# Eight heads of a decode step's forward part: sums of V with P times K as two products of 64 rows each

## The chip, the cores and the metric

The kernel runs on one core of one Trainium2 chip. The metric is the device time of one execution in microseconds (us); of the kernel before there are three such times, 1683.71, 1685.32 and 1685.54, with the median 1685.32.

## The reference

The kernel computes the forward and the backward of one decode step: layer norm, attention of one query per batch row over a cache of 4096 keys and values, an output projection with a residual, a second layer norm and a gated feed-forward block. It returns the output and the gradients, those of the K and V caches among them. Cut to what matters:

```python
B, Sq, D = 4, 1, 512;  H, Sk, Dh = 32, 4096, 128;  F = 1792
q = (layernorm(x) @ wq) as (B, H, 1, Dh)
scores = einsum("bhqd,bhkd->bhqk", q, k_cache) * Dh ** -0.5
p = softmax(scores)
o = einsum("bhqk,bhkd->bhqd", p, v_cache)
h = x + o @ wo
out = h + swiglu(layernorm(h), w1, w3, w2)
# and the vjp of out for grad_out: gradients of x, k_cache, v_cache, wq, wo, w1, w3, w2
```

There are 4 x 32 = 128 pairs of batch row and head, called heads here. Each has 1 MB of K and 1 MB of V in bf16.

## The kernel before

**Stages.** A forward part walks over the 128 heads and reads all of K and V (256 MB); it ends at about 660 us. A short middle part does the feed-forward block, forward and backward. The backward part reads V again and writes the gradients of K and V, 1 or 2 MB per transfer, until the end.

**Slots.** K, V, transposed K and P times K all live in one arena of 23 slots of about 1 MB each (`Slot`). A load is issued on the queue of SyncE (SP) as soon as a slot is given back. So the number of loads under way depends on how soon the engines release slots. One slot in every 16 heads goes for good to the results `M_of(s)`.

**What a head needs.** For head s, `T_pe` (TensorE, a quarter) and `T_dve` (VectorE, the rest) transpose K. `S_head` makes the scores in PSUM. The softmax goes through `sm_max`, `sm_max_T`, `sm_gmax`, `sm_bcast`, `sm_exp`, `sm_sum`, `sm_norm` and `sm_P`, for two heads at once. `PK_pairs` (GpSimd) and `PK_mul` (VectorE, line 460) multiply K by P. `M_mm` (line 475) sums over the 4096 keys the product of V with [P times K, P]: 32 matmuls, each with a 128x128 piece of V as weights and 130 columns of P times K, into one PSUM tile `M_ps` of 128x130. Its first 128 columns serve the gradients later, its 129th is the attention output. `M_end` adds up the rows of P times K with eight matmuls (line 485), lets ScalarE copy the tile to the arena (line 489), and gives the slots of P times K and V back. The pool `psM` has two buffers, both of tag "M".

**Order of the work.** The forward loop runs over 64 groups `gi` of two heads. Its order is written out by hand, and each engine runs its instructions in that order. In group gi the scores are those of heads 2gi and 2gi+1. The sums of V are those of two earlier heads: m1 = 2gi - 3 and m2 = 2gi - 2. On VectorE a group is, in order: `sm_max`, a transpose for the next group, `sm_gmax`, a transpose, the copy `nm` of `sm_exp` (line 422), the place of M_end(m1), two transposes, the reciprocal of `sm_norm`, PK_mul(pk1), the place of M_end(m2), a transpose of 1024 words (`T_dve(nb, 2, 2)`), and PK_mul(a). The part of the loop around the two M_end:

```python
        sm_exp(gi)
        if has1:
            M_end(m1)
...
        if has2:
            M_mm(m2, 24, SJ)
            M_end(m2)
            load_V(m2 + VQ)
...
            T_dve(nb, 2, 2)
        PK_mul(a)
```

Every 16 heads `O_cols` (lines 505 and 507) follows M_end(m1); its first copy on VectorE reads what ScalarE's copy of M_end(m1) has just written. Every 32 heads `kP_flush` follows too. Both are in the kernel before and after.

Of the kernel before, what the change touches and what calls it, by code (L numbers as in the profile page):

```python
# [9 lines left out]
FP32 = mybir.dt.float32  # L10
BF16 = mybir.dt.bfloat16
ALU = mybir.AluOpType
# [10 lines left out]
NPAIR = 8  # L23
OLD = 9
LEAD = 64


@with_exitstack
def kernel(
# [22 lines left out]
    nc = tc.nc  # L52
    P = nc.NUM_PARTITIONS
# [5 lines left out]
    Dh = A_k_cache.shape[3]  # L59
# [6 lines left out]
    SJ = Sk // P  # L66
# [3 lines left out]
    PKW = Dh + 2  # L70
# [55 lines left out]
    class Slot:  # L126
        def __init__(self, name, src=free):
# [5 lines left out]
            self.w = arena[:, self.i * SLOT:(self.i + 1) * SLOT]  # L133
            o = (self.i + 1) % 2 * LEAD
            self.t = self.w[:, o:o + SJ * Dh]
# [13 lines left out]
    class Slot2:  # L149
# [5 lines left out]
        def __init__(self):  # L155
            self.i = min(self.choices())[1]
            free.remove(self.i)
            free.remove(self.i + 1)
            self.t = arena[:, self.i * SLOT + LEAD:(self.i + 2) * SLOT]

# [56 lines left out]
    def ones_window(col):  # L217
        i = col % 2
        return onesw[i][:, 32 - i - col:64 - i - col]
# [80 lines left out]
    with ExitStack() as c0:  # L300
# [11 lines left out]
        for h in range(H):  # L312
            for cc in range(DC):
                nc.tensor.matmul(qT_ps[:, h, :], lhsT=wq_s[cc].b(HD)[:, h * Dh:(h + 1) * Dh], rhs=xhatT[:, cc, :],
                                 start=(cc == 0), stop=(cc == DC - 1))
# [4 lines left out]
        for r in range(2):  # L320
            for t_ in range(2):
                for q in range(4):
                    nc.tensor.matmul(qr_ps[32 * q:32 * (q + 1), 2 * r + t_, :], lhsT=ident_b[:, 64 * r + t_:64 * (r + 1):2],
                                     rhs=qT_bf[:], start=True, stop=True, tile_position=(0, 32 * q))
# [5 lines left out]
    def M_of(s):  # L330
        return Ms[s // MC].w[:].bitcast(FP32)[:, 0:MC * (Dh + 1)].rearrange("p (n c) -> p n c", c=Dh + 1)[:, s % MC, :]
# [3 lines left out]
    psM = c1.enter_context(tc.tile_pool(name="psM", bufs=2, space=bass.MemoryType.PSUM))  # L335
# [13 lines left out]
    hold = {}  # L349
# [103 lines left out]
    def PK_pairs(s):  # L453
        PKs[s] = Slot("PK")
        PK = PKs[s].w[:].rearrange("p (j c) -> p j c", c=PKW)
        nc.gpsimd.tensor_copy(out=PK[:, :, Dh:PKW], in_=P_all[:, s, :, None].to_broadcast([P, SJ, 2]))  # L456

    def PK_mul(s):
        PK = PKs[s].w[:].rearrange("p (j c) -> p j c", c=PKW)
        nc.vector.tensor_tensor(  # L460
            out=PK[:, :, 0:Dh].rearrange("p j (r t) -> p j r t", t=2),
            in0=Ks[s].heads().rearrange("p j (r t) -> p j r t", t=2),
            in1=PK[:, :, None, Dh:PKW].to_broadcast([P, SJ, Dh // 2, 2]),
            op=ALU.mult,
        )
        Ks.pop(s).give()
        kdone["n"] += 1

    def M_mm(s, j0, j1):
        if j0 == 0:  # L470
            hold["M"] = psM.tile([P, PKW], FP32, name="M_ps", tag="M")
        PK = PKs[s].w[:].rearrange("p (j c) -> p j c", c=PKW)
        Vn = Vs[s].heads()
        for j in range(j0, j1):
            nc.tensor.matmul(hold["M"][:], lhsT=Vn[:, j, :], rhs=PK[:, j, :], start=(j == 0), stop=(j == SJ - 1))  # L475

    def M_end(s):
        w = s % 32
        PK = PKs[s].w[:].rearrange("p (j c) -> p j c", c=PKW)
        if w == 0:  # L480
            hold["kP"] = psK.tile([P, 4, Dh], FP32, name="kP_ps", tag="kP")
        for c in range(2):
            for q in range(4):
                j0 = (c * 4 + q) * 4
                nc.tensor.matmul(hold["kP"][32 * q:32 * (q + 1), :, :], lhsT=ones_window(w), rhs=PK[:, j0:j0 + 4, 0:Dh],  # L485
                                 start=(w == 0 and c == 0), stop=(w == 31 and c == 1), tile_position=(0, 32 * q))
        if s % MC == 0:
            Ms.append(Slot("M"))
        nc.scalar.copy(out=M_of(s), in_=hold["M"][:, 0:Dh + 1])
        PKs.pop(s).give()  # L490
        Vs.pop(s).give()

# [160 lines left out]
    for gi in range(NGI):  # L653
        nxt = gi < NGI - 1
        a, na, nb = gi * G, gi * G + 2, gi * G + 3
# [6 lines left out]
        if has1:  # L662
            M_mm(m1, 0, 16)
# [6 lines left out]
        if has1:  # L670
            M_mm(m1, 16, SJ)
# [5 lines left out]
        if has1:  # L677
            M_end(m1)
            load_V(m1 + VQ)
            if m1 % 32 == 31:  # L680
                kP_flush(m1)
            if m1 % MC == MC - 1 and m1 < NH - 1:
                O_cols(m1 - MC + 1, m1 + 1)
# [15 lines left out]
        if has2:  # L699
            M_mm(m2, 0, 24)  # L700
        sm_P(gi)
# [4 lines that stand above are left out]
# [21 lines left out]
    PK_pairs(NH - 1)  # L727
    M_mm(NH - 3, 0, SJ)
    M_end(NH - 3)
    PK_mul(NH - 1)  # L730
    weights(NGI)
# [118 lines left out]
    with ExitStack() as cm:  # L850
# [40 lines left out]
        for wi, wt in enumerate((w1, w3)):  # L891
            for fc in range(FC):
                for cc in range(DC):
                    nc.tensor.matmul(gu_ps[:, wi, fc, :], lhsT=w13_view(wt, cc)[:, fc * P:(fc + 1) * P], rhs=hhatT[:, cc, :],
                                     start=(cc == 0), stop=(cc == DC - 1))
            if wi == 0:
# [13 lines left out]
                                in1=of4[:, :, None].to_broadcast([NH, B, Dh]), op=ALU.mult)  # L910
# [13 lines left out]
        for jj in range(DC):  # L924
            i_mm = 0
            for (lt, wt) in ((d_gateT_bf, w1), (d_upT_bf, w3)):
                for fc in range(FC):
                    nc.tensor.matmul(dn_ps[:, jj, :], lhsT=w13_view(wt, jj)[:, fc * P:(fc + 1) * P], rhs=lt[:, fc, :],
                                     start=(i_mm == 0), stop=(i_mm == 2 * FC - 1))
# [16 lines left out]
        for s in range(3):  # L946
# [8 lines left out]
                         start=True, stop=True)  # L955
# [5 lines left out]
                                       in1=hhatT_f[:], op0=ALU.mult, op1=ALU.mult)  # L961
        nc.vector.tensor_tensor(out=u[:], in0=u[:], in1=z[:, 0], op=ALU.add)
        nc.vector.scalar_tensor_tensor(out=u[:], in0=m[:, 0, None, :].to_broadcast([P, DC, B]), scalar=-1.0 / D,
                                       in1=u[:], op0=ALU.mult, op1=ALU.add)
# [5 lines left out]
        for b0, b1 in ((0, 1), (1, B)):  # L970
            ps = psA.tile([P, B, Dh], FP32, tag="rT", name="rep_ps")
            for b in range(b0, b1):
                for jj in range(DC):
                    nc.tensor.matmul(ps[:, b, :], lhsT=dhT[:, jj, b:b + 1].to_broadcast([P, P]), rhs=wo_page(0)[:, 0, jj, :],
                                     start=(jj == 0), stop=(jj == DC - 1))
# [12 lines left out]
    with ExitStack() as c2:  # L988
# [544 lines left out]
        for t in range(NT):  # L1533
            s = SP + 2 * t
# [46 lines left out]
```

## Time and profile before

| | |
|---|---|
| median of the three runs | 1685.32 us |
| the profiled execution's own time | 1683.33 us |
| its span, first to last instruction | 1681.5 us |
| busy: TensorE, VectorE, ScalarE, GpSimd | 74%, 74%, 57%, 25% of the span |
| data moved | 707.16 MB, 421 GB/s in the mean |
| the 128 `M_mm`: TensorE | 4096 matmuls, 285.9 us busy |
| the 128 `PK_mul`: VectorE | 292.4 us busy, 2285 ns each |
| span 240 to 260 us: TensorE, VectorE busy | 17.29 and 19.00 of 20 us |

The profile gives busy time, idle time and what ended it ("releaser", named by engine, tile and line). A line such as L475 is a line of the kernel before. PE is TensorE's matmuls, PEld its weight loads, DVE VectorE, ACT ScalarE, POOL GpSimd, SP SyncE. The timeline lists instructions in order of time: start and length in us, engine, line, operation, output and input, count, and in brackets the idle time before and what ended it.

### The profile page before, as it was taken

What the parts mean: (1) busy time and instruction counts of PE and PEld (TensorE: products, weight loads), DVE (VectorE), ACT (ScalarE), POOL (GpSimd) and SP (SyncE); (2) the same over time, 40 slices, a digit from 0 to 9 for tenths busy, and PEclk for the clock granted to TensorE, in tenths of its full rate; (3) what the DMA queues carried; (4) which work ended last, traced back from release to release, by engine and by line L of the source; (5) the groups of instructions that cost most, each with busy time, mean ns of one, the idle gap of its engine ahead of it and who ended that gap; (6) DMA issues with size and microseconds to landing.
All of it is one profiled execution on the core that took longest, in us unless ns stands there. A gap on an engine that the chain in (4) does not pass through costs nothing.

```text
span 1681.5 us, 33231 instructions
## 1 busy us (share of the span) xinstructions
PE 1243.9 (74%) x13784; PEld 874.1 (52%) x13784; DVE 1238.8 (74%) x1204; ACT 957.5 (57%) x1482; POOL 412.9 (25%) x732
## 2 busy tenths in 40 slices
PE   5889888888888888877777657567766776776750
PEld 4777776667666776644433335444444443444430
DVE  5989899999999987767766467576655656655682
ACT  3455454445445544677666556666665676676650
POOL 1221222222232223444552323211100011111110
PEclk9999999999999999999999878886667667676675
DMA  9999999999999999999999999999999999999996
GB/s 401 424 425 425 425 424 425 424 425 424 418 424 412 424 404 407 412 409 425 426 426 428 430 430 429 429 430 430 430 430 429 431 429 431 430 429 429 431 431 277
DMA packets 80983, 707.16 MB, mean 421 GB/s; under 512 B 8748, under 2 KB 12984, under 8 KB 15296
## 3 DMA queue, kind: packets, MB, share of 16 engines
q1 hardware_dynamic: 80416, 704.94, 99.4%
q8 instruction: 108, 1.77, 0.4%
q14 instruction: 43, 0.35, 0.0%
q0 software_dynamic: 416, 0.10, 0.0%
HBM read 422.59 MB, written 282.34 MB: 419 GB/s over the span
## 4 chain that ended last, share of the span: by engine, by line
DMA 40%; DVE 8%; PE 5%; ACT 4%; issue 3%; POOL 2%; DVEq 0%; SPq 0%; ACTq 0%; POOLq 0%
DMA out_dram<-arena 37%; DVE arena L1434 6%; ACT arena L806 3%; DMA arena<-in_A_v_cache_dram 3%; POOL zd L1246 1%; PE pt_tps L805 1%; PE M_ps L475 1%; DVE arena L460 1%; PE dq_ps L1032 1%; PE dP_ps L1280 1%; DMA arena<-arena 0%; PE pt_wo L613 0%; POOL P L1251 0%; ACT Pn L439 0%; POOL arena L1431 0%
## 5 line engine op out<-in xcount | busy, mean ns | idle before, releaser
L806 ACT COPY arena<-pt_tps 128x1024 bf16<-128x1024 bf16 x512 | 491.1, 1026 | 239.2 <-PE pt_tps L805 236.1
L805 PE MATMUL pt_tps<-ident_f,arena 128*128 128x128 f32 x2048 | 397.0, 346 | 195.4 <-DMA arena<-in_A_v_cache_dram 111.7
L805 PEld LDWEIGHTS pt_tps<-ident_f,arena 128*128 128x128 f32 x2048 | 290.8, 175 | 362.7 <-issue 187.3
L1434 DVE TENSOR_TENSOR arena<-arena 128x8192 bf16<-128x8192 bf16 x48 | 212.4, 4425 | 206.6 <-DMA out_dram<-arena 176.3
L475 PE MATMUL M_ps<-arena 128*128 128x130 bf16 x4096 | 285.9, 222 | 43.7 <-DMA arena<-in_A_v_cache_dram 43.2
L460 DVE TENSOR_TENSOR arena<-arena 128x4096 bf16<-128x4096 bf16 x128 | 292.4, 2285 | 24.3 <-POOL arena L456 24.3
L475 PEld LDWEIGHTS <-arena 128*128 128x128 bf16 x4096 | 252.3, 99 | 65.1 <-DMA arena<-in_A_v_cache_dram 58.1
L1434 DVE TENSOR_TENSOR arena<-dS,arena 128x8192 bf16<-128x8192 bf16 x48 | 212.4, 4426 | 63.6 <-DMA out_dram<-arena 63.6
L367 DVE STREAM_TRANSPOSE arena<-arena 128x512 f32<-128x512 f32 (+1 forms) x321 | 250.5, 796 | 0.0
L362 ACT COPY arena<-pt_tps 128x1024 bf16<-128x1024 bf16 x128 | 129.4, 1012 | 189.4 <-PE pt_tps L361 147.4
L373 POOL TENSOR_TENSOR W<-qrep,wmask 128x128 bf16<-128x128 bf16 x128 | 120.0, 938 | 85.6 <-PE S_ps L393 71.2
L1431 POOL COPY arena<-arena 128x128 bf16<-128x128 bf16 x48 | 45.2, 941 | 374.5 <-DVE arena L1434 248.6
L456 POOL COPY arena<-P_all 128x64 bf16<-128x64 bf16 x128 | 32.4, 253 | 413.1 <-ACT P_all L450 410.0
L1343 POOL COPY arena<-arena 64x4 bf16<-64x4 bf16 x96 | 78.5, 818 | 127.7 <-PE dP_ps L1363 118.2
L1363 PE MATMUL dP_ps<-arena 128*32 128x512 bf16 x768 | 85.3, 478 | 8.4 <-ACT arena L806 7.9
L450 ACT COPY P_all<-pt_P 32x64 bf16<-32x64 bf16 x256 | 51.9, 203 | 54.6 <-PE pt_P L446 52.4
L820 DVE TENSOR_TENSOR arena<-dS,arena 128x4096 bf16<-128x4096 bf16 x32 | 73.3, 2292 | 12.7 <-DMA out_dram<-arena 12.3
L361 PE MATMUL pt_tps<-ident_b,arena 128*128 128x128 bf16 x1024 | 80.5, 223 | 0.0
L820 DVE TENSOR_TENSOR arena<-P,arena 128x4096 bf16<-128x4096 bf16 x29 | 66.4, 2293 | 18.4 <-DMA out_dram<-arena 17.3
L485 PE MATMUL kP_ps<-arena,onesw 128*32 128x512 bf16 x1024 | 79.6, 388 | 0.0
L393 PE MATMUL S_ps<-arena,W 128*32 128x256 bf16 x1536 | 75.2, 286 | 0.5 <-DVE arena L367 0.2
L439 ACT ACTIVATE Pn<-E,rl 128x1024 bf16<-128x1024 f32 x64 | 73.7, 1151 | 3.2 <-DVE rl L436 3.2
(257 smaller groups left out, 1402.3 us busy)
## 6 DMA issues: line engine op xcount, KB each, us to landing
out_dram<-arena SPq DMA_DIRECT2D x96, 2048.0 KB, 27.5
arena<-in_A_v_cache_dram SPq DMA_DIRECT2D x160, 1024.0 KB, 15.9
arena<-in_A_k_cache_dram SPq DMA_DIRECT2D x128, 1024.0 KB, 15.5
arena<-in_A_v_cache_dram SPq DMA_DIRECT2D x48, 2048.0 KB, 31.7
out_dram<-arena SPq DMA_DIRECT2D x72, 1024.0 KB, 19.8
arena<-in_A_wq_dram SPq DMA_DIRECT2D x8, 1024.0 KB, 17.8
arena<-in_B_w_dram SPq DMA_DIRECT2D x8, 896.0 KB, 14.9
out_dram<-arena SPq DMA_DIRECT2D x6, 896.0 KB, 26.5
```

What stands on the lines that cost most here:

```text
L361: nc.tensor.transpose(pt[:, i, :], Kn[:, c * GW + i, :], ident_b[:])
L362: nc.scalar.copy(out=KT[:, c * GW:(c + 1) * GW, :], in_=pt[:])
L367: nc.vector.transpose(out=KT[:, c * w_:(c + n) * w_], in_=Kn[:, c * w_:(c + n) * w_])
L373: nc.gpsimd.tensor_tensor(out=W[:, hl], in0=qrep[:, :, s:s + 1].to_broadcast([P, 4, 32]), in1=wmask[:, hl, None, :].to_broadcast([P, 4, 32 ...
L460: nc.vector.tensor_tensor(out=PK[:, :, 0:Dh].rearrange("p j (r t) -> p j r t", t=2), in0=Ks[s].heads().rearrange("p j (r t) -> p j r t", t=2),
L475: nc.tensor.matmul(hold["M"][:], lhsT=Vn[:, j, :], rhs=PK[:, j, :], start=(j == 0), stop=(j == SJ - 1))
L485: nc.tensor.matmul(hold["kP"][32 * q:32 * (q + 1), :, :], lhsT=ones_window(w), rhs=PK[:, j0:j0 + 4, 0:Dh], start=(w == 0 and c == 0), stop ...
L805: nc.tensor.transpose(ptw[:, jj, :], w[:, 4 * g + jj, :], ident_f[:])
L806: nc.scalar.copy(out=v.rearrange("p (j d) -> p j d", d=Dh)[:, g * GW:(g + 1) * GW, :], in_=pt[:])
L820: nc.vector.tensor_tensor(out=dst.rearrange("p j (r t) -> p j r t", t=2), in0=col2[:, :, None, :].to_broadcast([P, SJ, Dh // 2, 2]), in1=r ...
L1363: nc.tensor.matmul(rows["acc"][32 * c:32 * (c + 1), :], lhsT=zt[t % B][:, k, ZP - m:ZP - m + 32], rhs=words_of(v, 2 * c + u, k), start=(pl ...
L1434: nc.vector.tensor_tensor(out=dst.rearrange("p (j r t) -> p j r t", r=Dh // 2, t=2), in0=col2[:, :, None, :].to_broadcast([P, 2 * SJ, Dh / ...
```

## The change

For heads 40 to 47 (`HALVES`) the 128 rows of the contraction are split. Each of the 32 steps becomes two matmuls, one over partitions 0 to 63 of V and of P times K, one over partitions 64 to 127, each placed in its own 64 rows of the array. The first sums into `M_ps`, the second into a second PSUM tile `Mh_ps`, taken from the same pool. After ScalarE's copy of `M_ps` VectorE adds the 129 columns of `Mh_ps` to the copied row. The other 120 heads are as before. The order of all other instructions on all engines, and of all transfers, is the same.

```diff
+HALVES = range(40, 48)
...
     def M_mm(s, j0, j1):
         if j0 == 0:
             hold["M"] = psM.tile([P, PKW], FP32, name="M_ps", tag="M")
+            if s in HALVES:
+                hold["Mh"] = psM.tile([P, PKW], FP32, name="Mh_ps", tag="M")
         PK = PKs[s].w[:].rearrange("p (j c) -> p j c", c=PKW)
         Vn = Vs[s].heads()
         for j in range(j0, j1):
+            if s in HALVES:
+                for a, M in enumerate((hold["M"], hold["Mh"])):
+                    r_ = slice(64 * a, 64 * (a + 1))
+                    nc.tensor.matmul(M[:], lhsT=Vn[r_, j, :], rhs=PK[r_, j, :], start=(j == 0), stop=(j == SJ - 1),
+                                     tile_position=(64 * a, 0))
+                continue
             nc.tensor.matmul(hold["M"][:], lhsT=Vn[:, j, :], rhs=PK[:, j, :], start=(j == 0), stop=(j == SJ - 1))
...
         nc.scalar.copy(out=M_of(s), in_=hold["M"][:, 0:Dh + 1])
+        if s in HALVES:
+            nc.vector.tensor_tensor(out=M_of(s), in0=M_of(s), in1=hold["Mh"][:, 0:Dh + 1], op=ALU.add)
```

## The prediction

> **What bounds the kernel now.** I read the slices of the page first, then the timelines of VectorE, ScalarE and TensorE around heads 40 to 47, then the waits and the chain behind them.
>
> ```profile
> span 1681.5 us, 33231 instructions
> DMA  9999999999999999999999999999999999999996
> GB/s 401 424 425 425 425 424 425 424 425 424 418 424 412 424 404 407 412 409 425 426 426 428 430 430 429 429 430 430 430 430 429 431 429 431 430 429 429 431 431 277
> ```
>
> The DMA engines are full nearly everywhere: at about 425 GB/s the four 1 MB loads of a group take 4.194 MB / 425 GB/s = 9.87 us. But VectorE is nearly as full, and its timeline shows what a group costs by computation alone:
>
> ```profile
> 247.66 0.16 DVE L422 COPY nm<-b_ps 128x1 f32<-128x1 f32 x1 [0.21 <-PE b_ps L417]
> 247.74 1.29 DVE L367 STREAM_TRANSPOSE arena<-arena 128x512 f32<-128x512 f32 x2
> 249.04 2.27 DVE L460 TENSOR_TENSOR arena<-arena 128x4096 bf16<-128x4096 bf16 x1
> 251.23 1.24 DVE L367 STREAM_TRANSPOSE arena<-arena 128x1024 f32<-128x1024 f32 x1
> 252.72 2.29 DVE L460 TENSOR_TENSOR arena<-arena 128x4096 bf16<-128x4096 bf16 x1 [0.26 <-POOL arena L456]
> ...
> 276.86 0.16 DVE L422 COPY nm<-b_ps 128x1 f32<-128x1 f32 x1 [0.21 <-PE b_ps L417]
> 277.86 0.17 DVE L505 COPY OT_f<-arena 128x16 f32<-128x16 f32 x1 [0.85 <-ACT arena L489]
> 278.16 1.30 DVE L367 STREAM_TRANSPOSE arena<-arena 128x512 f32<-128x512 f32 x2
> 282.77 2.25 DVE L460 TENSOR_TENSOR arena<-arena 128x4096 bf16<-128x4096 bf16 x1
> ```
>
> ```profile
> 238.64 0.26 ACT L489 COPY arena<-M_ps 128x129 f32<-128x129 f32 x1
> 242.67 0.27 ACT L489 COPY arena<-M_ps 128x129 f32<-128x129 f32 x1
> 248.38 0.26 ACT L489 COPY arena<-M_ps 128x129 f32<-128x129 f32 x1
> 277.58 0.26 ACT L489 COPY arena<-M_ps 128x129 f32<-128x129 f32 x1
> 288.13 0.25 ACT L489 COPY arena<-M_ps 128x129 f32<-128x129 f32 x1
> ```
>
> The copies of odd heads (39 at 238.64, 41 at 248.38) come 9.74 us apart, so a group takes 9.74 us, with only 0.21 + 0.26 = 0.47 us of idle VectorE. The second block is group 25, where `O_cols` puts a VectorE copy behind ScalarE's copy of head 47: VectorE stands still for 0.85 us, transposes behind it wait, and the group (277.58 to 288.13) takes 10.55 us, 0.81 more. That is a price for exactly the wait that the change adds for odd heads.
>
> From 606 us to 697, where the first gradient goes out, computation sets the pace; the chain of waits has no transfer in it there:
>
> ```profile
> 623.65 2.29 DVE arena L460
> 627.04 0.94 PE M_ps L475 x16
> ```
>
> After 725 us the transfers are full to the end. So lost time counts if the forward part is still late by it when the gradients begin; the transfers then have stood still for as long.
>
> **Part 1: the matmuls.** Eight heads get 32 more matmuls and weight loads each, 256 of both.
>
> ```profile
> 248.78 1.56 PE L475 MATMUL M_ps<-arena 128*128 128x130 bf16 x24
> 251.90 0.62 PE L485 MATMUL kP_ps<-arena,onesw 128*32 128x512 bf16 x8
> 13.15 3.49 PE L314 MATMUL qT_ps<-xhatT,arena 128*128 128x4 bf16 x125 [2.24 <-DMA arena<-in_A_wq_dram]
> ```
>
> 24 full matmuls take 1.56 us with 0.22 us (the length of one) for the last, so one starts every 1.34 / 23 = 58 ns. No row has matmuls side by side in different rows of the array. The nearest is L485, side by side in four groups of columns: 8 matmuls of 512 columns in 0.62 us, where one after another they would need 8 x 58 x 512/130 = 1.8 us. L314 shows that a 128x128 weight load with a tiny matmul needs only 3.49 / 125 = 28 ns, so two loads per step (56 ns) fit within 58 ns. Bounds: 0, or 32 x 58 ns = 1.86 us a head if the halves run one after another. I take 0, the row nearest in kind.
>
> The Trainium skill ("TensorE: Matmul & The Clock Gate", Part 3) states for row groups what no row of this trace shows: matmuls in different ones start about 4 ns apart. By it this term would be 0.
>
> Entering and leaving a differently divided array may cost. Full to columns: the last matmul of L475 starts at 251.75, that of L485 at 251.90, 0.09 us above the usual step; columns to full shows 0.23 us of "issue" before L475. For m2 such gaps hide: `sm_P` waits 0.54 us for ScalarE anyway, and ScalarE's copy of M stands behind its copies of P by 0.45 us. For m1 the second half of `M_mm` lies on the path to `nm`: two switches of 0.1 to 0.23 us. I take 0.2 us for each of four odd heads: **0.8 us** (0 to 2).
>
> The Trainium skill ("TensorEngine Tiling (Array Packing)", Key Properties) speaks against the change here: another tiling mode drains TensorE. If a drain were the full 0.22 us of a matmul, two switches for each of four heads would make it 1.8 us by an estimate from that page; the 0.09 us above shows less.
>
> **Part 2: the adds.** The row nearest to an add of 128x129 from PSUM and SBUF is
>
> ```profile
> L1056 DVE TENSOR_TENSOR arena<-pt_dqf,arena 128x128 f32<-128x128 f32 x1 | 0.3, 292 | 0.4 <-PE pt_dqf L1052 0.4
> ```
>
> so 0.29 us each. The wait in front costs more, as VectorE keeps its order.
> - Even head 40 (group 21): VectorE would start the 1024-word transpose at 241.49; the copy of M ends at 242.67 + 0.27 = 242.94. Stall, add, transpose end near 244.4, and PK_mul(a), before at 242.99, follows: **+1.4 us**. Queued behind are that transpose, PK_mul(a) and `sm_max`; `S_head` of the second head waits for the transpose, and GpSimd's `W` for `S_head`.
> - Odd heads alone: as `O_cols`, +0.8. Groups 22, 23 and 24 have both kinds. From `nm` on: the transposes start 1.2 us later; the reciprocal makes Pn, and so the copy of the even head's M, 0.73 us later (in group 25 that copy comes 282.33 - 276.86 = 5.47 after `nm`, in group 20 242.67 - 237.93 = 4.74). The add starts 5.76 after `nm`, PK_mul(a) at 7.18, where it was 252.72 - 247.66 = 5.06: **+2.1 us**, three times.
> - Head 47 (group 25) already has that wait: **+0.3 us**.
>
> Together 1.4 + 6.3 + 0.3 = **8.0 us**. Both buffers of `psM` now belong to one head, but each add is done before the `S_head` or 24-step `M_mm` ahead of the next use, so I add nothing.
>
> **Part 3: the clock.** TensorE idles 1.4 to 2.1 us more before `S_head` of the second head. One stall of 1.81 us shows what may follow (a line of the timeline, and one of the table of windows, whose third last column is the granted clock):
>
> ```profile
> 599.41 2.78 PE L475 MATMUL M_ps<-arena 128*128 128x130 bf16 x24 [1.81 <-DMA arena<-in_A_v_cache_dram]
> 600.00:602.00 2.00, 2.00 (x22) 2.00 (x20) 2.00 (x2) 0.23 (x1) 0.00 (x0) 0.50 1.00 422
> ```
>
> The granted clock fell to 0.50, and 24 matmuls took 2.78 us. `S_head`, half of `M_mm` and `T_pe` at half speed would cost 1.95 us, less the 0.87 us that TensorE waits for `mxm`: 1.1 us a group, in none to four groups. I take one, the end nearer to group 25, where 1.17 us of idleness left the clock at 1.00: **1.1 us** (0 to 4.4).
>
> **Part 4: what is given back.** By 290 us the computation is 8.0 + 0.8 + 1.1 = 9.9 us late. Transfers go on: a load lands 17 us after issue there, 14 to 15 us between 450 and 600, and 5 us with an empty queue (gradients at 692 to 710), so lateness up to about 9 us only shortens the queue. From 290 to 606 us the kernel before sometimes waits for V (32.4 us of TensorE's idle time, mostly hidden). Summed over the groups above 9.74 us, or above what flush and `O_cols` cost (11.70 and 10.55), this makes 3.8 us, 1.86 of them the group at 597 (12.41). A late computation doesn't wait there: **-3.8 us**. Later nothing gives it back: groups without waits for V take 9.74 to 9.78.
>
> Sum: 9.9 - 3.8 = +6.1 us. On the profiled execution's own 1683.33 (span 1681.5 and 1.8 around it) that is 1689.4; that run lies 2.0 us under the median 1685.32, so I predict **1691.4**.
>
> **Rivals.**
> - *One after another* (chance 0.17): the halves don't overlap. The second half of `M_mm` of m1 delays `nm` by 0.93 us and the first by some 0.15; head 40 gets 0.8 through `sm_P`. 8.0 + 0.8 + 4 x 1.1 = 13.2 us late, less 3.8, with or without clock: 9 to 14 us, so 1694 to 1699. For it: no row shows row halves. Against it: L485.
> - *The queue covers it* (chance 0.18): no loss. Place: the loads between 290 and 697 us. Price of the adds: up to 10 us late, but all given back, if the waits for V are worth more than the 3.8 counted or the gradients at 697 find loads enough to bridge (5 us of queue there). It decides where lateness at 606 us falls under about 3 us. For it: 32.4 us of waits for V. Against it: no transfer in the chain after 623. Time 1684 to 1688.
> - *Faster* (0.05): the later loads miss the dips of the transfers at 461, 534, 604 and 720 us, worth some 3 to 4 us in all: 1681.
> - *No split takes place*: the built order of instructions has the 256 matmuls and 8 adds, so no.
>
> **How the numbers follow.** A measurement of this kernel tells 0.2%, 3.4 us, from no change. The forecast, +3.4 to +9, has 0.60. Slower: 0.60 + 0.17 = 0.77; same 0.18; faster 0.05. The range leaves out the faster case and the far end of the serial one: 1685 to 1698.
>
> **What would show it.** Eight adds of about 0.29 us, waiting for ScalarE's copy of M: about 1.4 us at head 40, 0.85 at 41, 43 and 45, about 1.0 at 42, 44 and 46. Copies of odd heads 41 to 47 some 11.5 to 12 us apart; `M_mm` of these heads with 64 matmuls in the time of 32; fewer waits for V until 606 us, none of 1.8 at 599; the first gradient some 6 us later than 697, and a longer dip of the transfers before it. Wrong if 24 steps take 2.9 us (serial), or if the first gradient goes out at 697 as before.

## The result and the profile after

The changed kernel takes 1690.35 us (median of 6 runs, 1689.22 to 1691.25). Beside it on the same chip the kernel before took 1684.82 us. The ratio is 1.0033, with a 95% interval of 1.002 to 1.0046: 5.5 us slower. The profiled execution of the changed kernel took 1691.25 us, the slowest of its six; that of the kernel before took 1683.33 us, below the median of its kernel. Between these two traces there are 7.9 us to find, more than between the medians.

In the kernel after, a line number is higher by one from line 26 on and by more further down: ScalarE's copy of M is L498, the add L500, a matmul of a half L481, a full one L484, PK_mul L461, the transposes L368, `nm` L423.

First the slices of the page of the kernel after (40 equal slices of the span):

```profile
span 1689.5 us, 33751 instructions
DMA  9999999999999999999999999999999999999996
GB/s 401 424 425 425 425 424 406 424 414 420 417 424 412 415 408 410 373 408 426 426 426 428 428 432 429 430 430 428 431 429 429 431 429 430 430 430 429 430 430 277
```

The DMA row is what it was; the change can be seen only in the bytes. Slice 7 (253 to 296 us) moved 406 GB/s where it moved 425, and slice 17 (676 to 718 us) 373 where it moved 412.

Next VectorE's timeline after, head 40 and then heads 41 and 42 (start, length, engine, line, operation, operands; in brackets the idle time before and what ended it):

```profile
243.08 0.29 DVE L500 TENSOR_TENSOR arena<-arena,Mh_ps 128x129 f32<-128x129 f32 x1 [1.40 <-ACT arena L498]
...
249.19 0.16 DVE L423 COPY nm<-b_ps 128x1 f32<-128x1 f32 x1 [0.31 <-PE b_ps L418]
250.20 0.29 DVE L500 TENSOR_TENSOR arena<-arena,Mh_ps 128x129 f32<-128x129 f32 x1 [0.85 <-ACT arena L498]
250.41 1.30 DVE L368 STREAM_TRANSPOSE arena<-arena 128x512 f32<-128x512 f32 x2
...
254.88 0.29 DVE L500 TENSOR_TENSOR arena<-arena,Mh_ps 128x129 f32<-128x129 f32 x1 [0.94 <-ACT arena L498]
255.09 1.24 DVE L368 STREAM_TRANSPOSE arena<-arena 128x1024 f32<-128x1024 f32 x1
256.25 2.25 DVE L461 TENSOR_TENSOR arena<-arena 128x4096 bf16<-128x4096 bf16 x1
```

Each add takes 0.29 us, but VectorE stands still in front of it, for 1.40 us with head 40, 0.85 us with an odd head and 0.94 us with a later even one, until ScalarE's copy is done. The transposes and PK_mul, which need nothing of that copy, stand behind. What this does to a group is seen in ScalarE's copies of odd heads (39, 41, 43, 45, 47 and 49; the same view as before):

```profile
238.76 0.26 ACT L498 COPY arena<-M_ps 128x129 f32<-128x129 f32 x1
...
249.91 0.26 ACT L498 COPY arena<-M_ps 128x129 f32<-128x129 f32 x1
...
261.71 0.26 ACT L498 COPY arena<-M_ps 128x129 f32<-128x129 f32 x1
...
273.50 0.26 ACT L498 COPY arena<-M_ps 128x129 f32<-128x129 f32 x1
...
285.30 0.26 ACT L498 COPY arena<-M_ps 128x129 f32<-128x129 f32 x1
...
296.17 0.26 ACT L498 COPY arena<-M_ps 128x129 f32<-128x129 f32 x1
```

The five groups take 11.15, 11.80, 11.79, 11.80 and 10.87 us in place of 9.74 four times and 10.55, so 1.41 + 2.06 + 2.05 + 2.06 + 0.32 = 7.9 us more. Head 49 is copied at 296.17, where it was 288.13.

TensorE's timeline shows the halves:

```profile
245.14 0.23 PE L481 MATMUL M_ps<-arena 64*128 64x130 bf16 x1
245.14 0.23 PE L481 MATMUL Mh_ps<-arena 64*128 64x130 bf16 x1
245.21 0.22 PE L481 MATMUL M_ps<-arena 64*128 64x130 bf16 x1
245.21 0.22 PE L481 MATMUL Mh_ps<-arena 64*128 64x130 bf16 x1
```

Two halves start together and the next pair follows some 0.06 us later. The 24 pairs of head 40 take 1.58 us, where 24 full matmuls took 1.56. With heads 42, 44 and 46 one half starts 0.17 us ahead of all the rest, and the 24 pairs take 1.75 us; blocks of 16 pairs take 1.11 us, where 16 full matmuls took 1.10 or 1.11.

At last the table of windows, which finds the lost time (columns: window; its length; busy time and instructions of PE, PEld, DVE, ACT, POOL; granted clock; DMA share; GB/s). The kernel before:

```profile
280.00:400.00 120.00, 101.36 (x1698) 83.38 (x1699) 112.14 (x147) 59.66 (x135) 31.92 (x72) 1.00 1.01 425
690.00:780.00 90.00, 68.19 (x544) 39.38 (x540) 63.54 (x57) 63.01 (x72) 40.80 (x65) 0.96 1.00 411
```

The kernel after:

```profile
280.00:400.00 120.00, 101.40 (x1726) 82.90 (x1729) 111.58 (x149) 59.22 (x134) 31.70 (x72) 1.00 1.00 413
690.00:780.00 90.00, 70.68 (x647) 44.86 (x645) 61.22 (x63) 64.45 (x76) 39.76 (x61) 0.92 0.96 393
```

From 280 to 400 us it moved 12 GB/s less, or 1.44 MB, which is 3.4 us at 425 GB/s; from 690 to 780 us 18 GB/s less, or 1.62 MB, 3.8 us at 429. Together that is 7.2 of the 7.9 us. In the first window the loss lies in two short stretches: 383 and 390 GB/s from 280 to 300 us, behind the late groups, and 392 to 411 from 360 to 390 us, behind the `kP_flush` of head 63; from 300 to 360 us the rate is the full 424 to 426. From 780 to 1600 us both move 429 GB/s: the backward part only repeats the lateness it is given.

The chain from the add to these two places is then: a stalled VectorE keeps slots from coming free, so loads are issued later (a 1 MB load of V issued between 370 and 400 us lands 8.9 us later, where it was 16.1: the queue is shorter); the first transfers of gradients go out later as well. On SyncE's queue:

```profile
705.13 16.16 SPq L842 DMA_DIRECT2D out_dram<-arena  x7
```

In the kernel before this first line stood at 697.44.

### The profile page after: what moved, and what is told of

Same layout as the page of the kernel before. It is cut to its first block, busy times and chain, and to the rows that moved or that the text cites. A ratio compares the mean times of both kernels' runs of the same rounds, so it can differ in the third digit from the quotient of the medians.

```text
span 1689.5 us, 33751 instructions
## 1 busy us (share of the span) xinstructions
PE 1252.8 (74%) x14040; PEld 879.0 (52%) x14040; DVE 1239.4 (73%) x1212; ACT 958.2 (57%) x1482; POOL 414.8 (25%) x732
## 4 chain that ended last, share of the span: by engine, by line
DMA 36%; PE 7%; DVE 7%; ACT 6%; issue 2%; POOL 2%; DVEq 0%; SPq 0%; ACTq 0%
DMA out_dram<-arena 30%; DVE arena L1445 5%; DMA arena<-in_A_v_cache_dram 5%; ACT arena L817 5%; PE pt_tps L816 2%; PE dq_ps L1043 1%; DMA arena<-arena 1%; PE dP_ps L1291 1%; POOL zd L1257 1%; PE M_ps L484 1%; POOL arena L1040 1%; DVE arena L461 1%; PE pt_w L615 1%; PE pt_wo L624 0%; POOL P L1262 0%
## 5 line engine op out<-in xcount | busy, mean ns | idle before, releaser
L461 DVE TENSOR_TENSOR arena<-arena 128x4096 bf16<-128x4096 bf16 x128 | 292.2, 2283 | 21.4 <-POOL arena L457 20.0
L484 PE MATMUL M_ps<-arena 128*128 128x130 bf16 x3840 | 267.4, 222 | 9.4 <-DMA arena<-in_A_v_cache_dram 9.3
L484 PEld LDWEIGHTS <-arena 128*128 128x128 bf16 x3840 | 238.5, 99 | 25.5 <-DMA arena<-in_A_v_cache_dram 12.3
L368 DVE STREAM_TRANSPOSE arena<-arena 128x512 f32<-128x512 f32 (+1 forms) x321 | 250.6, 797 | 0.0
L457 POOL COPY arena<-P_all 128x64 bf16<-128x64 bf16 x128 | 32.4, 253 | 412.7 <-ACT P_all L451 409.7
L426 ACT ACTIVATE E<-S_ps,nm 128x256 f32<-128x256 f32 x64 | 30.3, 474 | 96.6 <-DVE nm L423 96.6
```

Of the source, the lines that this page charges most:

```text
L368: nc.vector.transpose(out=KT[:, c * w_:(c + n) * w_], in_=Kn[:, c * w_:(c + n) * w_])
L461: nc.vector.tensor_tensor(out=PK[:, :, 0:Dh].rearrange("p j (r t) -> p j r t", t=2), in0=Ks[s].heads().rearrange("p j (r t) -> p j r t", t=2),
```

## The experiments

My theory: the time is the wait of VectorE for ScalarE's copy, with what stands behind it on VectorE, and neither the split of the matmuls nor the 0.29 us of an add. The rivals: the split itself costs; the work of the adds costs; the DMA queue covers a small lateness. Each was timed beside the kernel before, which took 1684.05 us (median) beside the first four of them (the later adds, the split without adds, the wait alone, the even heads) and 1684.14 us beside the others.

**The same adds, later in VectorE's order.** The addition of an odd head is issued after the two transposes, that of an even head after the 1024-word transpose. Head 47's alone stays, as `O_cols` reads its sum.

```diff
-        if s in HALVES:
-            nc.vector.tensor_tensor(out=M_of(s), in0=M_of(s), in1=hold["Mh"][:, 0:Dh + 1], op=ALU.add)
+        if s == HALVES[-1]:
+            M_add(s)
...
+        if has1 and m1 != HALVES[-1]:
+            M_add(m1)
...
+        if has2:
+            M_add(m2)
         PK_mul(a)
```

> The split matmuls and the eight adds stay; seven adds are issued later on VectorE: those of 41, 43 and 45 behind the two transposes that follow, those of the even heads behind the transpose of 1024 words. By then ScalarE's copy is done. Theory 'wait' (VectorE standing in front of ScalarE's copy is the cost): no stall before these adds, only 8 x 0.29 us of work, partly in the 0.47 us that VectorE idles per group; groups of heads 41 to 47 at 9.8 to 10.3 us instead of 11.15 to 11.8; the first gradient within 1.5 us of the kernel before (0.6 to 2.5 us of lateness, most of it given back), time within 1.5 us of before. Rival 'split' (the matmuls of 64 rows, their switches or the second bank cost the time): still 5 us over before, groups still near 11.8.

Measured: 1685.73 us, ratio 1.0009 (1.0 to 1.0017). VectorE's timeline of this kernel shows the adds of heads 41 and 42:

```profile
249.39 0.25 DVE L506 TENSOR_TENSOR arena<-arena,Mh_ps 128x129 f32<-128x129 f32 x1
...
253.14 0.29 DVE L506 TENSOR_TENSOR arena<-arena,Mh_ps 128x129 f32<-128x129 f32 x1
```

They have no bracket: nothing was waited for. Groups take 10.03 us in place of 11.8. Of the 2.06 us that a group had gained in length, 1.77 were place in the order and not work. What is left of the loss is 1.7 us of 5.5. That is a little more than I expected (1.5), as is the first gradient, 2.0 us later than in the kernel before.

**The split without adds.** The second half of the sums of eight heads is missing here.

```diff
-        if s in HALVES:
-            nc.vector.tensor_tensor(out=M_of(s), in0=M_of(s), in1=hold["Mh"][:, 0:Dh + 1], op=ALU.add)
```

> The split matmuls stay, the adds are left out, so the second half of the sums of eight heads is missing from the result. Theory 'wait': groups 9.75 to 9.95 us (two switches of the array, about 0.1 us a group), time within 1 us of before. Rival 'split': +4 to +6 us, groups near 11.8.

Measured: 1685.74 us, ratio 1.001 (1.0001 to 1.0019). Groups take 9.84 us, 0.10 more than before, and all of it stands in front of `nm` (0.31 us of waiting, before 0.21). GB/s of the two windows: 425 and 411, as before. So in this trace the split costs 0.1 us a group. The median is 1.7 us over that of the kernel before, where I expected at most 1; that is not found in this trace, whose execution took 1684.64 us, and it stays unexplained. It is near what single runs of the kernel before differ by (1682.97 to 1686.02), and as large as with the later adds. That the split costs up to 1.7 us of time is thus not ruled out by the medians; next to the adds in place it is the smaller part.

**The wait without the split.** All matmuls as before; in place of the add, a maximum of M with itself at the same place, with the same wait.

```diff
+        if s in HALVES:
+            nc.vector.tensor_tensor(out=M_of(s), in0=M_of(s), in1=hold["M"][:, 0:Dh + 1], op=ALU.max)
```

> The matmuls of the kernel before, unsplit; for heads 40 to 47 VectorE takes the maximum of the copied row and of M_ps itself behind ScalarE's copy: the same instruction size, place and wait as the add, with no other value. Theory 'wait': groups 11.1 to 11.8 us as with the change, time +4.5 to +6.5 us over before. Rival 'split': groups 9.75 to 10.0, time within 1 us of before.

Measured: 1690.62 us, ratio 1.004 (1.0027 to 1.0052). VectorE's timeline, heads 40 to 42:

```profile
243.50 0.29 DVE L492 TENSOR_TENSOR arena<-arena,M_ps 128x129 f32<-128x129 f32 x1 [1.40 <-ACT arena L490]
...
250.51 0.29 DVE L492 TENSOR_TENSOR arena<-arena,M_ps 128x129 f32<-128x129 f32 x1 [0.85 <-ACT arena L490]
...
255.19 0.29 DVE L492 TENSOR_TENSOR arena<-arena,M_ps 128x129 f32<-128x129 f32 x1 [0.94 <-ACT arena L490]
```

The stalls are those of the changed kernel to the hundredth. The time is 6.6 us over the kernel before (0.1 above what I expected), where the change costs 5.5; the two intervals overlap. The groups are longer by 1.31, 1.95, 1.96, 1.95 and 0.33 us, 7.5 in all; the split adds the other 0.4 of 7.9. So the wait alone, with no split and no second PSUM tile, is enough for the loss. This run, with the two above, shows the cause.

**Even heads alone, odd heads alone.**

```diff
-HALVES = range(40, 48)
+HALVES = range(40, 48, 2)
```

> The change for heads 40, 42, 44 and 46 alone. Theory 'wait' with the prices of the prediction: four groups of +1.4 us (11.15), lateness 5.6 us at 290 us, less the 2.7 us that the changed kernel got back until 606 us: +2 to +4 us. Rival 'queue' (lateness up to some 9 us is covered by loads under way, what counts is only what exceeds it): within 1 us of before.

```diff
-HALVES = range(40, 48)
+HALVES = range(41, 48, 2)
```

> Only the odd heads 41, 43, 45 and 47 have the two halves and the add. Theory (the time is VectorE's wait behind ScalarE's copy, and it only counts once computation is later than what the V loads leave free): +0.85 us of stall in each of groups 21 to 24, so copies of odd heads 10.6 us apart in three or four groups, 2.5 to 3.3 us later at head 49, about +0.3 to +0.8 us at head 127, time +0 to +2 us. Rival (the halves or an extra instruction cost by themselves, whatever they wait for): no stall in the trace, or a shift at head 49 that isn't the sum of the stalls.

Measured: even heads 1688.95 us, ratio 1.0028 (1.0018 to 1.0038), four groups of 11.05 us, 1.31 more each; odd heads 1685.78 us, ratio 1.0007 (0.9998 to 1.0016), three groups of about 10.57, 0.83 more each. 1.31 + 0.83 = 2.14 is near the 2.06 of both, so the two waits add up. The even heads are 5.2 us late at head 49 and cost 4.9 us of time, so a lateness of 5 us is not covered by the queue. The time is more than the +2 to +4 us that I expected: the groups are as forecast, and the lateness at head 127 is down to 2.5 us, but the first gradient is again 5.2 us later than in the kernel before. The odd heads are 3.1 us late at head 49, 0.5 us at head 127, and 1.6 us in the median, as expected, with an interval that reaches below zero: what the queue covers, if anything, is 1 to 2 us, and the even heads don't show even that.

**Thirty-two heads.**

```diff
-HALVES = range(40, 48)
+HALVES = range(40, 72)
```

> Heads 40 to 71 have the two halves and the add, 16 groups in place of 4. Theory (about 2.06 us a group, of which 1.9 to 2.8 us in all are given back by waits for V that go): 14 or 15 groups x 2.06 us, about +31 us at head 71, +28 to +32 us in time, no V wait after head 45. Rival (the DMA queue or a later part takes up a fixed share of the lateness, so that the first four groups are dearer or cheaper than the rest): the price of a group changes along the way, or the time grows by less than 24 us.

Measured: 1715.32 us (two runs), ratio 1.0184 (1.0165 to 1.0202), 31.2 us more, as expected. Nearly all groups of the stretch take 11.81 us, the last as the first. The price is linear, and the transfers show where it is paid (table of windows):

```profile
280.00:400.00 120.00, 93.77 (x2058) 71.85 (x2058) 96.77 (x145) 50.35 (x112) 26.38 (x60) 0.99 0.92 352
690.00:780.00 90.00, 74.61 (x882) 52.01 (x880) 58.89 (x75) 58.47 (x77) 41.42 (x88) 0.92 0.99 396
```

352 GB/s is nearly the 4.194 MB of a group in 11.81 us, 355 GB/s: once the queue is short, computation sets the rate of the transfers. A load of V lands after 5.1 us there (issued between 370 and 400 us), so the 16 us of the kernel before were about 11 us of queue. In the kernel with eight heads a load of V issued between 560 and 590 us lands after 10.8 us, where it was 14.1: the queue is still 3.3 us shorter near the end of the forward part, and 3.8 us of transfers are lost from 690 us on. The two numbers fit; that the one becomes the other was not tested by itself.

**The same wait taken out of the kernel before.** Nothing is split; the copies of `O_cols` go behind the next two transposes.

```diff
-            if m1 % MC == MC - 1 and m1 < NH - 1:
-                O_cols(m1 - MC + 1, m1 + 1)
...
+        if has1 and m1 % MC == MC - 1 and m1 < NH - 1:
+            O_cols(m1 - MC + 1, m1 + 1)
```

> The kernel before, nothing split; its own copies to OT_f (in seven groups up to head 111) are moved behind the next transposes on VectorE, so that they no longer stand behind ScalarE's copy of M. Theory (the same wait that the added adds have, taken out where the kernel before already had it): seven groups of 9.74 us in place of 10.55, up to 5.7 us of computation; but V is awaited for 32 us in all already, so that most of it becomes waiting for V. Time -0.5 to -2 us. Rival (the copies' wait is hidden anyway): within 0.5 us of before. On the other side: transposes of the next head have to wait less, nothing is seen that could make it over 1 us slower.

Measured: 1684.33 us, ratio 1.0001 (0.9992 to 1.001): no change. The group of head 49 takes 9.73 us in place of 10.55, and that of head 81 9.71 in place of 10.56. But the group after head 81 takes 11.29 where it took 10.46: it waits for V. That is the rival's figure (within 0.5 us); the -0.5 us at the near end of my theory is inside the interval, its -2 us is not. The same 0.8 us is worth nothing where it is taken away and costs where it is added: here the computation was not earlier than V let it be. This was also the one version that might have beaten both kernels; none did.

**The kernel before once more**, for a second trace of it.

> The kernel before, nothing changed, for a second profile of it. If the granted clock at 680 to 700 us differs between executions of one kernel, this profile shows a clock below 1.00 there as the changed kernels did, and the first gradient goes out 1 to 2 us later than at 697.44; if it belongs to the change, the profile repeats 1.00 up to 690 us and 697.4 us within 0.3.

Measured: 1684.36 us. The granted clock does differ between executions of the same program. Window 600 to 605 us, first in the first trace of the kernel before:

```profile
600.00:605.00 5.00, 5.00 (x81) 4.43 (x79) 3.25 (x3) 1.31 (x6) 0.24 (x1) 0.75 0.98 378
```

and in the second:

```profile
600.00:605.00 5.00, 4.46 (x87) 3.50 (x85) 5.00 (x3) 2.14 (x6) 1.24 (x2) 1.00 1.02 421
```

The clock of 0.75 is gone, and the group of 12.41 us takes 10.56; TensorE's matmuls wait 13.4 us for V between 290 and 610 us in place of 32.4. In the first trace TensorE had stood idle for 1.81 us there, in the second for 0.65. The slow group is not a matter of one execution only: with `O_cols` moved, TensorE idles for 1.73 us at the same place, the next 24 matmuls take 2.78 us again, and the group takes 12.41. In the second trace the clock is 0.78 from 680 to 685 us, where it was 1.00. The first gradient goes out at 697.69, 27.1 us after the copy of head 127, where it was 25.9 in the first trace (697.44 less 671.57, where the forward part thus ends): half of my expectation came (a clock under 1.00), the 1 to 2 us of delay of the first gradient did not.

**All of them by bytes.** The two windows of the first comparison, read in the same way from every profile (the loss is worked out as above, against 425 and 411 GB/s; the last column is the profiled execution's time above 1683.33 us):

| kernel | late at head 49 | GB/s, 280 to 400 and 690 to 780 us | lost there | first gradient later | time |
|---|---|---|---|---|---|
| changed | 8.0 us | 413, 393 | 7.2 us | 7.7 us | +7.9 us |
| wait alone | 8.1 | 412, 397 | 6.6 | 7.3 | +7.3 |
| even heads | 5.2 | 417, 394 | 5.8 | 5.2 | +5.6 |
| odd heads | 3.1 | 422, 405 | 2.1 | 1.9 | +2.6 |
| later adds | 1.7 | 424, 405 | 1.5 | 2.0 | +2.6 |
| split without adds | 0.3 | 425, 411 | 0.0 | 0.6 | +1.3 |
| before once more | 0.8 | 425, 410 | 0.2 | 0.3 | +1.0 |

Lateness of the computation, bytes that were not moved and time go together within about 1.5 us in every row. The first gradient tells the time best, within 0.8 us. The execution in the first trace of the kernel before was some 1 us below the median of its kernel, so about 1 us of each time is not the edit's.

## Why the prediction was right, and where it was not

The forecast was 6.1 us more; 5.5 were measured between the medians. The sign, the mechanism and the size were right, the size in part by luck, as the steps show:

- **Matmuls (0): right.** The halves of a pair start within 0.01 us of each other, in the three longer blocks one step of 0.06 us apart; one after another, 24 pairs would have taken 2.9 us and took 1.58 to 1.75. The Trainium skill ("TensorE: Matmul & The Clock Gate", Part 3) has row groups starting within about 4 ns; the trace agrees, as far as its steps of 0.01 us can tell.
- **Switches (0.8): too high, 0.4 measured** (7.9 less 7.5 with the wait alone), 0.1 us for each odd head. From the rows I had read 0.1 to 0.23 us for each of a head's two switches; the two together took 0.10. The Trainium skill ("TensorEngine Tiling (Array Packing)", Key Properties) says that another tiling mode drains TensorE; a full drain would be twice the 0.22 us of a matmul per odd head by the estimate made ahead, and the runs show 0.10 us.
- **Adds and waits (8.0): right, 7.5.** 1.31 for 1.4, 1.95 for 2.1 three times, 0.33 for 0.3. The stalls came as forecast: 1.40, then 0.85 and 0.94 (for "about 1.0").
- **Clock (1.1): wrong, 0 where it was placed.** The clock was 1.00 from 236 to 284 us. TensorE was busy for only 7.4 of the 10 us from 270 on, and that did not lower it.
- **Lateness at 290 us: 7.9, for 9.9,** by the three terms above.
- **Given back (3.8): too high.** Against the first trace of before, lateness fell from 8.0 at head 49 to 5.3 at head 127, so 2.75. Against the second it fell from 7.3 to 6.3, so 1.0. All 32.4 us of waits for V did go, but most of them had been hidden. The term contained the 12.41 us group as something that the kernel before always has; its second trace does not have it. The two errors, 2.0 us too late and 1.0 to 2.8 us too much given back, cancelled in the sum by luck.
- **"Lateness up to about 9 us only shortens the queue": wrong in part.** 3.4 us of transfers were lost by 400 us, while loads still landed 9 us after their issue. A transfer without a queue takes 5 us, and of the 16 us only 11 are cover. Even 8 us of lateness, less than these 11, cost bytes: at two moments the rate fell, behind the late groups and behind the flush of head 63, and between them it was full.
- **"Later nothing gives it back": right.** The groups of both kernels after 606 us are alike (9.8 us), and the transfers at 690 to 780 us lose 3.8 us. That the first gradient went 7.7 us later and not 6 lies between head 127 and it: 28.3 us there, against 25.9 and 27.1 in the two traces of before. For this stretch the forecast had no term. In all ten traces its length goes along with the granted clock in it: 25.9 us at 0.93 (first trace of before, `O_cols` moved), 26.8 to 27.3 at 0.87 (second trace of before, split without adds, odd heads, 32 heads), 27.7 and 27.8 at 0.82 (later adds, wait alone), 28.3 and 28.6 at 0.76 and 0.75 (changed kernel, even heads). That the clock makes the length was not tested by itself. A late forward part is not needed for a low clock (the later adds are 0.1 us late at head 127) and does not always bring one (the 32 heads are 30.7 us late there, at 0.87); what sets it stays open.
- **Rivals.** One after another: refuted by the pairs. The queue covers it: refuted by the even heads, 5.2 us late and 4.9 us slower, and by the 32 heads. Faster: nothing in any trace moved that way.

## What to carry to other kernels

Cost a small operation by what it waits for and by what stands behind it on an engine that keeps its order: here 2.3 us of adds stood behind 7.6 us of stalls (0.85 of them, at head 47, were there before), and moving the same adds one or two instructions down took most of the loss away. Where transfers and computation are both nearly full, compare the bytes moved in a few long windows of two traces: they show where the time was lost even where the busy share does not. Such a kernel is not symmetric: computation made earlier only waited for its loads, computation made later was paid for, here with 0.7 to 1 us of time (between medians) for each us of lateness at the end of the changed heads, from 5 us on.

## What the runs showed of the hardware

- Pairs of 64-row matmuls with 130 columns, each with its own weight load, went nearly as fast as single 128-row ones: 24 pairs in 1.58 us (1.75 where the first half started 0.17 us early) against 1.56, though the number of matmuls and weight loads doubled.
- Stalls of VectorE of 0.85 to 1.40 us in each of four groups in a row left TensorE's granted clock at 1.00, while an idle time of 1.81 us of TensorE in the kernel before was followed by 0.50. In its second trace TensorE idled for 0.65 us at the same place, and the clock stayed at 1.00.
- DMA's busy share was 1.00 in a window that moved 413 GB/s and 1.01 in one that moved 425: the share alone does not tell a loss of 3%. From 290 to 300 us it was 1.01 at 390 GB/s and 1.01 at 424.
